# A decode attention step with its gradients and a gated MLP: the MLP moved whole to the front, weights laid out with neighbouring rows on a partition

## The chip, the core and the metric

The kernel runs on one core of a Trainium2 chip. The metric is device time in microseconds. Three runs of the kernel before took 745.66 to 747.29 us, median 746.24 us.

## What is computed

One token `x` (1 x 640) is normalised, goes through attention over a cache of 32 heads x 8192 positions x 128, and beside it through a gated MLP with 1728 hidden units. The output is the sum, and the kernel also returns the gradients of it, for a given `grad_out`, with respect to x, both caches and all five weight matrices.

```python
def _A_ref(x, k_cache, v_cache, wq, wo):
    q = (x @ wq).reshape(B, Sq, Hq, Dh).transpose(0, 2, 1, 3)
    scores = jnp.einsum("bhqd,bhkd->bhqk", q, k) * (Dh ** -0.5)
    p = _softmax(scores, axis=-1)
    o = jnp.einsum("bhqk,bhkd->bhqd", p, v)
    return o.transpose(0, 2, 1, 3).reshape(B, Sq, Hq * Dh) @ wo
...
xn = _layernorm(x, axis=-1)
return x + _A_ref(xn, k_cache, v_cache, wq, wo) + (silu(xn @ w1) * (xn @ w3)) @ w2
...
_out, _vjp = jax.vjp(_f, x, k_cache, v_cache, wq, wo, w1, w3, w2)
_grads = _vjp(grad_out)
```

All inputs and outputs are bf16. Each head reads 2 MB of K and 2 MB of V and writes 2 MB of dK and 2 MB of dV. wq and wo have 5.2 MB each, w1, w3 and w2 2.2 MB each, and each has a gradient of its own size.

## The kernel before

**Heads.** The outer loop (L480) is pipelined by one head: iteration h makes the scores of head h+1 and the outputs of head h. `product` (L271) forms S = K q and DP = V do: VectorE multiplies half a head of K or V by a row vector (L280), and TensorE sums over the head dimension by multiplying with the identity (L282). `outer` (L287) forms dV = p x do and dK = u x q in halves: VectorE makes 24 of 32 columns (L289), ScalarE the other 8 (L293), and Pool's queue issues the store (L295). `attend` (L326) and `dscores` (L345) contract V and K with one-column matmuls into `ob`.

**Loads.** All large loads go through SP's queue, in the order of the program. `load_k` and `load_v` (L108, L114) have three buffers each, so head h+3 is loaded once head h has been used (L503, L513). In front of the loop stand K0, wq and wo of group 0, V0, and K and V of heads 1 and 2 (L162 to L167).

**Groups.** Four heads share a group of wq and wo columns, loaded by `load_group` (L128) at the first head of the group before, into two buffers. `prep_steps` (L219) makes q (L224) and, by transposing wo (L234), do (L238) for the next group. `weights` (L348) uses a head's output vector: five one-column matmuls with wo (L357), then wo's buffer is overwritten with its own gradient on ScalarE (L359); the same for wq at the end of a group (L251). `finish_group` (L247) stores both. wq has 640 rows, of which a group is 1024 B each; a partition holds rows that lie 128 apart.

**The MLP.** It runs in four pieces of 432 hidden units. `load_piece` (L147) is called after heads 0, 5, 12 and 17, and `mlp_steps` (L377) is started at heads 3, 8, 15 and 20; its parts run in the gaps of the heads (`gap`, L472). A piece computes gate and up (L384), g times w2 (L387) and its sum (L390), some 15 small steps, a diagonal matrix (L430) from which TensorE and ScalarE make the row vectors broadcast to all partitions (L438, L441), the gradient of w2 in place (L443), and for w1 and w3 the product with the row vector (L452), its sum (L454) and the gradient in place (L456). The rows of w1 and w3 in a piece are 864 B long.

**Order.** VectorE, SP and Pool keep the order of the program (`ORDERED`, L58); the order of TensorE's and ScalarE's instructions is made by the framework's scheduler. `store` (L121) issues from Pool; stores of the last group but one and of the last MLP piece are put off (`late`) to head 30 (L487).

Of the kernel before, what the change touches and what calls it, by code (L numbers as in the profile page):

```python
# [9 lines left out]
BF16 = mybir.dt.bfloat16  # L10
F32 = mybir.dt.float32
# [5 lines left out]
P = 128  # L17
# [4 lines left out]
def kernel(  # L22
# [36 lines left out]
    NPIECE = 4  # L59
    ACT_J = 8  # L60
    scale = float(DH) ** -0.5
# [4 lines left out]
    mp = ctx.enter_context(tc.tile_pool(name="mlp", bufs=1))  # L66
# [14 lines left out]
    wq_v = A_wq.rearrange("(ci p) n -> p ci n", p=P)  # L81
    wo_v = A_wo.rearrange("(h p) c -> p h c", p=P)
    dwq_v = out_4.rearrange("(ci p) n -> p ci n", p=P)
    dwo_v = out_5.rearrange("(h p) c -> p h c", p=P)
    w1_v = B_w1.rearrange("(ci p) f -> p ci f", p=P)
    w3_v = B_w3.rearrange("(ci p) f -> p ci f", p=P)
    dw1_v = out_6.rearrange("(ci p) f -> p ci f", p=P)
    dw3_v = out_7.rearrange("(ci p) f -> p ci f", p=P)

    with tc.manual_schedule(engines=ORDERED):  # L90
# [7 lines left out]
        x_col_bf = consts.tile([P, NC], BF16, name="x_col_bf")  # L98
        g_col_bf = consts.tile([P, NC], BF16, name="g_col_bf")
        with nc.allow_non_contiguous_dma(reason="tiny column-layout loads of x / grad_out"):  # L100
            nc.sync.dma_start(x_col_bf[:], A_x.rearrange("a b (c p) -> p (a b c)", p=P))
            nc.scalar.dma_start(g_col_bf[:], grad_out.rearrange("a b (c p) -> p (a b c)", p=P))
# [25 lines left out]
        def load_group(g):  # L128
            hs = slice(g * GH * DH, (g + 1) * GH * DH)
            wq_g = wload.tile([P, NC, GH * DH], BF16, name="wq_g", tag="wq_g")  # L130
            nc.sync.dma_start(wq_g[:], wq_v[:, :, hs])
            wo_g = wload.tile([P, GH, D], BF16, name="wo_g", tag="wo_g")
            nc.sync.dma_start(wo_g[:], wo_v[:, g * GH:(g + 1) * GH, :])
            grp[g] = dict(wq=wq_g, wo=wo_g)

        assert F % NPIECE == 0
        FP = F // NPIECE
        pblocks = [(b0, min(P, FP - b0)) for b0 in range(0, FP, P)]
        NB = len(pblocks)
        NF = FP // P  # L140
        DRUN = 64
        DR1 = 48
        assert FP % DR1 == 0
        W1O, W3O, W2O = 0, NC * FP, 2 * NC * FP
        ml = {}

        def load_piece(pc):  # L147
            f0 = pc * FP
            wt = mp.tile([P, 2 * NC * FP + NB * D], BF16, name="wt", tag="wt")
            w1c = wt[:, W1O:W1O + NC * FP].rearrange("p (c f) -> p c f", c=NC)  # L150
            w3c = wt[:, W3O:W3O + NC * FP].rearrange("p (c f) -> p c f", c=NC)
            w2c = wt[:, W2O:W2O + NB * D].rearrange("p (b d) -> p b d", b=NB)
            if NB > NF:
                nc.gpsimd.memset(w2c[:, NF, :], 0.0)
            nc.sync.dma_start(w2c[:, 0:NF, :], B_w2[f0:f0 + NF * P, :].rearrange("(fb p) c -> p fb c", p=P))
            nc.sync.dma_start(w1c, w1_v[:, :, f0:f0 + FP])
            nc.sync.dma_start(w3c, w3_v[:, :, f0:f0 + FP])
            if NB > NF:
                nc.sync.dma_start(w2c[0:FP - NF * P, NF, :], B_w2[f0 + NF * P:f0 + FP, :])
            ml[pc] = (w1c, w3c, w2c)  # L160

        load_k(0)  # L162
        load_group(0)
        load_v(0)
        for h in range(1, min(3, H)):
            load_k(h)
            load_v(h)  # L167
# [18 lines left out]
        OUT0 = NC  # L186

# [3 lines left out]
        x_col = consts.tile([P, NC], F32, name="x_col")  # L191
        g_col = consts.tile([P, NC], F32, name="g_col")
# [5 lines left out]
        dxn_mlp = consts.tile([P, NC], F32, name="dxn_mlp")  # L198
        x_bc = tpool.tile([P, 2, D], F32, name="x_bc", tag="T")
# [10 lines left out]
        nc.vector.tensor_copy(x_col[:], x_col_bf[:])  # L210
        nc.vector.tensor_scalar(xn_col[:], x_col[:], negmean[:], rstd[:], ALU.add, ALU.mult)
        nc.vector.tensor_copy(XN_rep[:], xn_col[:].unsqueeze(2).to_broadcast([P, NC, P]))
        nc.vector.tensor_copy(g_col[:], g_col_bf[:])
        nc.vector.tensor_copy(G_rep[:], g_col[:].unsqueeze(2).to_broadcast([P, NC, P]))
        nc.vector.tensor_copy(xn_col_bf[:], xn_col[:])
        nc.vector.tensor_copy(xn2[:], xn_col[:].unsqueeze(2).to_broadcast([P, NC, 2]))


        def prep_steps(g):  # L219
# [24 lines left out]
            nc.scalar.copy(do_g[:].rearrange("p h d -> p (h d)"), ps_d[:])  # L244
            G_["do"] = do_g

        def finish_group(g):  # L247
            G_ = grp.pop(g)
            store(dwo_v[:, g * GH:(g + 1) * GH, :], G_["wo"][:], g == NG - 2)
            for ci in range(NC):  # L250
                nc.scalar.activation(G_["wq"][:, ci, :], G_["dqbc"][:].rearrange("p h d -> p (h d)"),  # L251
                                     ACTF.Copy, scale=xn_col[:, ci:ci + 1])
            store(dwq_v[:, :, g * GH * DH:(g + 1) * GH * DH], G_["wq"][:], g == NG - 2)
# [94 lines left out]
        def weights(st):  # L348
# [5 lines left out]
            odq_bf = small.tile([P, 2], BF16, name="odq_bf")  # L354
            nc.vector.tensor_copy(odq_bf[:], odq[:])
            for ci in range(NC):
                nc.tensor.matmul(accbank[:, OUT0 + ci:OUT0 + ci + 1], lhsT=G_["wo"][:, hh, ci * P:(ci + 1) * P],  # L357
                                 rhs=odq_bf[:, 0:1], start=False, stop=True, skip_group_check=True)
            nc.scalar.activation(G_["wo"][:, hh, :], g_bc_bf[:], ACTF.Copy, scale=odq[:, 0:1])  # L359
# [5 lines left out]
            for ci in range(NC):  # L365
                nc.tensor.matmul(accbank[:, DXN0 + ci:DXN0 + ci + 1], lhsT=wqT[:, ci * P:(ci + 1) * P],
                                 rhs=odq_bf[:, 1:2], start=False, stop=True, skip_group_check=True)
# [5 lines left out]
            if hh == GH - 1:  # L373
                finish_group(st.g)


        def mlp_steps(pc):  # L377
            f0 = pc * FP
            w1c, w3c, w2c = ml.pop(pc)
            gu_ps = ps_w.tile([P, 2, 8], F32, name="gu_ps", tag="w")  # L380
            for wi, wt in enumerate((w1c, w3c)):
                for bi, (b0, rows) in enumerate(pblocks):
                    for ci in range(NC):
                        nc.tensor.matmul(gu_ps[0:rows, wi, bi:bi + 1], lhsT=wt[:, ci, b0:b0 + rows],  # L384
                                         rhs=xn_col_bf[:, ci:ci + 1], start=(ci == 0), stop=(ci == NC - 1))
            T2 = tpool.tile([P, NB, D], BF16, name="T2", tag="T")
            nc.vector.tensor_tensor(T2[:], w2c, g_bc_bf[:].unsqueeze(1).to_broadcast([P, NB, D]), ALU.mult)  # L387
            dh_ps = ps_w.tile([P, NB, DRUN], F32, name="dh_ps", tag="w")
            for i in range(D // DRUN):
                nc.tensor.matmul(dh_ps[:], lhsT=ident_bf[:], rhs=T2[:, :, DRUN * i:DRUN * (i + 1)],  # L390
                                 start=(i == 0), stop=(i == D // DRUN - 1))
            yield
            gu = mp.tile([P, 2, NB], F32, name="gu")
            nc.vector.memset(gu[:], 0.0)
            for bi, (b0, rows) in enumerate(pblocks):
                if rows < P:
                    nc.vector.tensor_copy(gu[0:rows, :, bi:bi + 1], gu_ps[0:rows, :, bi:bi + 1])
            nc.vector.tensor_copy(gu[:, :, 0:NF], gu_ps[:, :, 0:NF])
            gate = gu[:, 0, :]
            up = gu[:, 1, :]  # L400
            th = mp.tile([P, NB], F32, name="th")
            nc.scalar.activation(th[:], gate, ACTF.Tanh, scale=0.5)
            yield
            dhc = mp.tile([P, NB], F32, name="dhc")
            nc.vector.tensor_reduce(dhc[:], dh_ps[:], AX.X, ALU.add)
            sig = mp.tile([P, NB], F32, name="sig")
            nc.vector.tensor_scalar(sig[:], th[:], 0.5, 0.5, ALU.mult, ALU.add)
            silu = mp.tile([P, NB], F32, name="silu")
            nc.vector.tensor_tensor(silu[:], gate, sig[:], ALU.mult)
            hcol = mp.tile([P, NB], F32, name="hcol")  # L410
            nc.vector.tensor_tensor(hcol[:], silu[:], up, ALU.mult)
            hcol_bf = mp.tile([P, NB], BF16, name="hcol_bf")
            nc.vector.tensor_copy(hcol_bf[:], hcol[:])
            for bi, (b0, rows) in enumerate(pblocks):
                for ci in range(NC):
                    nc.tensor.matmul(accbank[:, OUT0 + ci:OUT0 + ci + 1], lhsT=w2c[0:rows, bi, ci * P:(ci + 1) * P],
# [61 lines left out]
        for _ in prep_steps(0):  # L478
            pass
# [108 lines left out]
```

## Time and profile before

| | |
|---|---|
| runs, median (lowest to highest) | 746.24 us (745.66 to 747.29) |
| the profiled execution's own time | 747.42 us |
| its span, first to last instruction | 745.7 us |
| TensorE, VectorE, ScalarE, Pool busy | 75%, 86%, 62%, 13% |
| packets' time on the load queue / the store queue, share of 16 DMA engines | 49.7% / 49.5% |
| HBM read / written | 151.67 MB / 151.34 MB |
| granted TensorE clock, mean | 0.762 |

The span is the time between the first and the last instruction; the execution's own time has 1.7 us more around it. A group line of the profile names the source line, the engine, the operation, what is written and read, the shapes, the count, then the busy time in us, the mean of one in ns, and the idle time before. A DMA's issue takes well under 1 us on its queue; its data land later: 15.2 us for a K load, 15.7 us for a dK or dV store, 17.6 and 24.7 us for wq and wo loads (medians).

### The profile page before, as it was taken

The numbers are of one execution on the slowest core, as the hardware profiler recorded it, in microseconds if no ns is written. First come the engines' busy times: TensorE is split into PE (matmuls) and PEld (weight loads), VectorE is DVE, ScalarE is ACT, GpSimd is POOL, SyncE is SP. The second block draws the span as 40 slices with busy tenths as digits, with TensorE's granted clock in tenths as the row PEclk, the third lists the DMA queues.
The fourth block names the chain that finished last, engine by engine and source line by source line (L and its number), as shares of the span: only waits on it lengthen the run. The fifth ranks groups of instructions, "written<-read, shape, count | busy, mean of one in ns | idle before, by whom it ended". The sixth has DMA issues, their size and how long they took to land.

```text
span 745.7 us, 15906 instructions
## 1 busy us (share of the span) xinstructions
PE 561.7 (75%) x6444; PEld 327.8 (44%) x6451; DVE 639.4 (86%) x764; ACT 463.2 (62%) x1378; POOL 97.9 (13%) x172
## 2 busy tenths in 40 slices
PE   2788677878777887784887877777778765888872
PEld 1344354445454454442554444454444442544442
DVE  3799688997988979879588997988999877899993
ACT  3456656566775477663766566766477753766676
POOL 0010102111111101210102111110111200111312
PEclk9868857687887668777857688876798776985885
DMA  8999999999999999999999999999999999999997
GB/s 319 427 420 407 420 422 405 374 416 421 417 427 423 415 429 424 425 419 384 402 420 399 371 417 419 422 428 422 420 425 420 424 416 427 380 421 428 395 362 299
DMA packets 50205, 304.04 MB, mean 408 GB/s; under 512 B 5460, under 2 KB 21780, under 8 KB 25556
## 3 DMA queue, kind: packets, MB, share of 16 engines
q1 hardware_dynamic: 26612, 151.51, 49.7%
q0 software_dynamic: 22720, 151.35, 49.5%
q8 instruction: 50, 0.82, 0.4%
q10 hardware_dynamic: 800, 0.17, 0.1%
q14 instruction: 23, 0.19, 0.1%
HBM read 151.67 MB, written 151.34 MB: 406 GB/s over the span
## 4 chain that ended last, share of the span: by engine, by line
DMA 43%; DVE 28%; PE 17%; issue 7%; ACT 2%; SPq 1%; POOL 1%; POOLq 0%; DVEq 0%; ACTq 0%
DMA wo_g<-in_A_wo_dram 22%; DVE T L280 14%; DMA out_dram<-wq_g 9%; DVE ot L289 8%; PE psS L282 7%; DMA Kt<-in_A_k_cache_dram 6%; DMA out_dram<-ot 5%; PE psDP L282 3%; PE ob L326 2%; DMA wq_g<-in_A_wq_dram 1%; DVE S_sb L299 1%; PE ps_t L234 1%; ACT wt L443 1%; DVE DP_sb L333 1%; PE ps_d L238 1%
## 5 line engine op out<-in xcount | busy, mean ns | idle before, releaser
L282 PEld LDWEIGHTS <-ident_bf 128*128 128x128 bf16 x1024 | 123.7, 122 | 233.1 <-issue 183.7
L282 PE MATMUL psDP<-T,ident_bf 128*128 128x512 bf16 x512 | 177.2, 507 | 62.5 <-DVE T L280 62.5
L293 ACT ACTIVATE ot<-qs_g,Uf 128x128 bf16<-128x128 bf16 x512 | 153.9, 389 | 38.6 <-DVE Uf L343 26.0
L282 PE MATMUL psS<-T,ident_bf 128*128 128x512 bf16 x512 | 164.4, 476 | 16.5 <-DVE T L280 15.3
L280 DVE TENSOR_TENSOR T<-Kt,qs_g 128x4096 bf16<-128x4096 bf16 x64 | 146.4, 2289 | 26.5 <-DMA Kt<-in_A_k_cache_dram 9.8
L293 ACT ACTIVATE ot<-do_g,Pf 128x128 bf16<-128x128 bf16 x512 | 155.7, 390 | 9.3 <-DMA out_dram<-ot 8.6
L280 DVE TENSOR_TENSOR T<-Vt,do_g 128x4096 bf16<-128x4096 bf16 x64 | 146.0, 2281 | 0.0
L295 POOL DMA_DIRECT2D out_dram<-ot x128 | 68.8, 538 | 573.9 <-ACT ot L293 324.1
L289 DVE TENSOR_TENSOR ot<-do_g,P 128x3072 bf16<-128x3072 bf16 x64 | 112.3, 1755 | 8.6 <-DMA out_dram<-ot 7.4
L289 DVE TENSOR_TENSOR ot<-qs_g,U 128x3072 bf16<-128x3072 bf16 x64 | 112.0, 1752 | 4.9 <-DMA out_dram<-ot 4.9
L345 PEld LDWEIGHTS <-Kt 128*128 128x128 bf16 x2048 | 58.7, 99 | 17.6 <-issue 14.9
L359 ACT ACTIVATE wo_g<-g_bc_bf,odq 128x640 bf16<-128x640 bf16 x32 | 26.5, 827 | 59.7 <-PE accbank L357 59.7
L345 PE MATMUL ob<-U,Kt 128*128 128x1 bf16 x2048 | 57.5, 164 | 3.1 <-DVE U L340 2.8
L326 PEld LDWEIGHTS <-Vt 128*128 128x128 bf16 x2048 | 58.0, 99 | 0.0
L326 PE MATMUL ob<-P,Vt 128*128 128x1 bf16 x2048 | 56.7, 164 | 0.0
L369 ACT ACTIVATE dq_diag<-ident_bf,odq 128x128 bf16<-128x128 bf16 x32 | 12.9, 402 | 46.6 <-DVE odq L353 46.6
L236 ACT COPY woT<-ps_t 128x512 bf16<-128x512 bf16 x40 | 22.5, 581 | 24.4 <-PE ps_t L234 24.4
L299 DVE TENSOR_REDUCE S_sb<-psS 128x64 f32<-128x512 f32 x32 | 21.9, 685 | 18.1 <-PE psS L282 18.1
L234 PE MATMUL ps_t<-ident_bf,wo_g 128*128 128x128 bf16 x160 | 19.2, 257 | 19.8 <-DMA wo_g<-in_A_wo_dram 19.8
L311 ACT ACTIVATE E<-S_sb,negM 128x64 f32<-128x64 f32 x32 | 11.1, 347 | 33.9 <-DVE negM L308 33.9
L336 PE MATMUL sm<-rdot,ones_f 128*128 128x1 f32 x64 | 12.1, 258 | 20.7 <-DVE E L335 20.7
L303 PE MATMUL sm<-ident_f,mrow 128*128 128x128 f32 x64 | 18.7, 380 | 10.7 <-DVE mrow L301 10.5
(122 smaller groups left out, 502.2 us busy)
## 6 DMA issues: line engine op xcount, KB each, us to landing
out_dram<-ot POOLq DMA_DIRECT2D x128, 1024.0 KB, 15.7
Kt<-in_A_k_cache_dram SPq DMA_DIRECT2D x32, 2048.0 KB, 15.2
Vt<-in_A_v_cache_dram SPq DMA_DIRECT2D x32, 2048.0 KB, 12.9
wq_g<-in_A_wq_dram SPq DMA_DIRECT2D x8, 640.0 KB, 17.6
wo_g<-in_A_wo_dram SPq DMA_DIRECT2D x8, 640.0 KB, 24.7
out_dram<-wo_g POOLq DMA_DIRECT2D x8, 640.0 KB, 17.5
out_dram<-wq_g POOLq DMA_DIRECT2D x8, 640.0 KB, 17.1
wt<-in_B_w_dram SPq DMA_DIRECT2D x8, 540.0 KB, 25.3
```

What stands on the lines that cost most here:

```text
L234: nc.tensor.transpose(ps_t[:, hh * DH:(hh + 1) * DH], wo_g[:, hh, ci * P:(ci + 1) * P], ident_bf[:])
L236: nc.scalar.copy(woT[:], ps_t[:])
L280: nc.vector.tensor_tensor(T[:], src[:, :, ds_], vec[:, ds_].unsqueeze(1).to_broadcast([P, J, DHH]), ALU.mult)
L282: nc.tensor.matmul(ps[:], lhsT=ident_bf[:], rhs=T[:, :, RUN * i:RUN * (i + 1)], start=(half == 0 and i == 0), stop=(half == 1 and i == DHH ...
L289: nc.vector.tensor_tensor(ot[:, 0:JD], vec.rearrange("p (a b) -> p a b", b=2).unsqueeze(1).to_broadcast([P, JD, DH // 2, 2]), w2[:, j0:j0 ...
L293: nc.scalar.activation(ot[:, j].rearrange("p a b -> p (a b)"), vec, ACTF.Copy, scale=wf[:, half, j - JD:j - JD + 1])
L295: nc.gpsimd.dma_start(dst[h][:, j0:j0 + JH, :], ot[:].rearrange("p j a b -> p j (a b)"))
L299: nc.vector.tensor_reduce(st.S[:], st.ps["S"][:], AX.X, ALU.add)
L303: nc.tensor.matmul(st.sm[:, 8:8 + P], lhsT=mrow[:].to_broadcast([P, P]), rhs=ident_f[:], start=True, stop=True, skip_group_check=True)
L326: mm = nc.tensor.matmul(st.ob[:, 0:1], lhsT=st.V[:, j, :], rhs=st.P2[:, j, 0:1], start=(j == 0), stop=(j == J - 1), skip_group_check=True)
L345: nc.tensor.matmul(st.ob[:, 1:2], lhsT=st.K[:, j, :], rhs=st.U2[:, j, 0:1], start=(j == 0), stop=(j == J - 1), skip_group_check=True)
L359: nc.scalar.activation(G_["wo"][:, hh, :], g_bc_bf[:], ACTF.Copy, scale=odq[:, 0:1])
```

## The change

Three things change together.

1. **Layouts.** wq, w1 and w3 are viewed so that partition p holds rows 5p to 5p+4; wo so that a partition holds four neighbouring rows of a group; w2 so that each of 108 partitions holds 16 neighbouring rows. The columns of x and xn follow ("pm" forms beside "cm" ones), and they are made by 20 one-column matmuls from the broadcast rows rather than by two DMAs.
2. **Groups.** wq is loaded and stored for eight heads at a time (2048 B rows), wo still for four. As a partition of wo now holds rows of one head next to each other, o is spread by a selection matrix: per head a small ScalarE activation and one f32 matmul into `on_ps`, and once per group `finish_wo` with all 20 matmuls and four ScalarE copies. The wq stores of the last two groups are issued for each group.
3. **The MLP** is one piece, ahead of head 0. w2 lies in three output buffers (tag "o"), w1 and w3 in two of the three K buffers, so K1 and K2 are loaded after the MLP's stores. The pool `mlp` is gone.

```diff
-        load_k(0)
-        load_group(0)
-        load_v(0)
-        for h in range(1, min(3, H)):
-            load_k(h)
-            load_v(h)
+        for rows in (6, 5, 5):
+            w2c = opool.tile([P, rows, D], BF16, name="w2c", tag="o")
+            nc.sync.dma_start(w2c[0:FR], w2_v[:, r0:r0 + rows, :])
...
+        w1t = kvpool.tile([P, NC, F], BF16, name="w1t", tag="K")
+        nc.sync.dma_start(w1t[:], w1_v)
+        w3t = kvpool.tile([P, NC, F], BF16, name="w3t", tag="K")
+        nc.sync.dma_start(w3t[:], w3_v)
+        load_k(0)
+        load_wq(0)
+        load_wo(0)
+        load_v(0)
+        load_v(1)
+        load_v(2)
...
+        mlp = mlp_steps()
+        next(mlp)
+        next(mlp)
         for _ in prep_steps(0):
             pass
+        for _ in mlp:
+            pass
+        load_k(1)
+        load_k(2)
```

```diff
+    wq_v = A_wq.rearrange("(p ci) n -> p ci n", ci=NC)
+    wo_v = A_wo.rearrange("(g p r) c -> g p r c", p=P, r=GH)
+    w1_v = B_w1.rearrange("(p ci) f -> p ci f", ci=NC)
+    w2_v = B_w2.rearrange("(q r) c -> q r c", r=R2)
...
+        def finish_wo(g):
...
+            for r in range(GH):
+                for ci in range(NC):
+                    nc.tensor.matmul(accbank[:, OUT0 + ci:OUT0 + ci + 1], lhsT=wo_g[:, r, ci * P:(ci + 1) * P],
+                                     rhs=on_bf[:, r:r + 1], start=False, stop=True, skip_group_check=True)
+                nc.scalar.activation(wo_g[:, r, :], g_bc_bf[:], ACTF.Copy, scale=on[:, r:r + 1])
+            store(dwo_v[g], wo_g[:], g == NG - 2)
...
-            for ci in range(NC):
-                nc.tensor.matmul(accbank[:, OUT0 + ci:OUT0 + ci + 1], lhsT=G_["wo"][:, hh, ci * P:(ci + 1) * P],
-                                 rhs=odq_bf[:, 0:1], start=False, stop=True, skip_group_check=True)
-            nc.scalar.activation(G_["wo"][:, hh, :], g_bc_bf[:], ACTF.Copy, scale=odq[:, 0:1])
+            om = small.tile([P, GH], F32, name="om")
+            nc.scalar.activation(om[:], rmask[:], ACTF.Copy, scale=odq[:, 0:1])
+            nc.tensor.matmul(G_["on_ps"], lhsT=sel[:, hh, :], rhs=om[:], start=(hh == 0), stop=(hh == GH - 1),
+                             skip_group_check=True)
+            if hh == GH - 1:
+                finish_wo(st.g)
```

The MLP itself, its sums over w2 first (R2 = 16, FR = 108):

```diff
+            for r0, rows, w2c in w2_parts:
+                T2 = tpool.tile([P, rows, D], BF16, name="T2", tag="T")
+                nc.vector.tensor_tensor(T2[0:FR], w2c[0:FR], g_bc_bf[0:FR].unsqueeze(1).to_broadcast([FR, rows, D]), ALU.mult)
...
+            for wi, wt in enumerate((w1t, w3t)):
+                wr = wt[:].rearrange("p c (q r) -> p c r q", r=R2)
+                for r in range(R2):
                     for ci in range(NC):
+                        nc.tensor.matmul(gu_ps[0:FR, wi, r:r + 1], lhsT=wr[:, ci, r, :],
                                          rhs=xn_col_bf[:, ci:ci + 1], start=(ci == 0), stop=(ci == NC - 1))
...
+            for r0, rows, w2c in w2_parts:
+                for r in range(rows):
...
+                    nc.scalar.activation(w2c[0:FR, r, :], g_bc_bf[0:FR, :], ACTF.Copy, scale=hcol[:, r0 + r:r0 + r + 1])
+                nc.gpsimd.dma_start(dw2_v[:, r0:r0 + rows, :], w2c[0:FR])
...
+            for wi, (wt, dst) in enumerate(((w1t, dw1_v), (w3t, dw3_v))):
+                for c0 in range(0, NC, 2):
...
+                    nc.vector.tensor_tensor(T[:], wt[:, c0:c0 + n, :],
+                                            bc_sb[:, wi, :].unsqueeze(1).to_broadcast([P, n, F]), ALU.mult)
...
+                nc.gpsimd.dma_start(dst, wt[:])
```

At the end, dx is stored from its own tile in 10 B pieces on SP's queue, and the output row on ScalarE's.

## The prediction, made before the changed kernel had run

> **What bounds the kernel now.** I read the page's engine table first: VectorE 86%, TensorE 75%, no engine full. Then the page's slices, where the DMA row is:
>
> ```profile
> DMA  8999999999999999999999999999999999999997
> GB/s 319 427 420 407 420 422 405 374 416 421 417 427 423 415 429 424 425 419 384 402 420 399 371 417 419 422 428 422 420 425 420 424 416 427 380 421 428 395 362 299
> DMA packets 50205, 304.04 MB, mean 408 GB/s; under 512 B 5460, under 2 KB 21780, under 8 KB 25556
> ```
>
> The 16 DMA engines are busy from the second slice to the last but one, yet the bytes per second vary: busy engines carry 420 to 429 GB/s in most slices and 362 to 384 in a few. So the bound is the DMA engines' time, and some of it goes to something other than bytes. The windows view tells what (columns: stretch in us, its length, five engines' busy time and count, TensorE clock, DMA share, GB/s):
>
> ```profile
> 5.00:20.00 15.00, 6.54 (x32) 3.73 (x33) 8.29 (x14) 5.73 (x10) 0.00 (x0) 1.00 1.02 402
> 20.00:35.00 15.00, 10.96 (x49) 4.75 (x46) 11.11 (x11) 5.64 (x14) 0.00 (x0) 0.89 1.02 434
> 80.00:125.00 45.00, 32.48 (x312) 18.45 (x310) 33.82 (x47) 23.37 (x66) 5.30 (x9) 0.66 1.01 426
> 125.00:145.00 20.00, 15.55 (x175) 9.18 (x174) 19.61 (x24) 13.33 (x41) 4.81 (x7) 0.67 0.98 358
> 405.00:425.00 20.00, 15.42 (x173) 9.04 (x171) 19.57 (x25) 13.11 (x41) 4.83 (x7) 0.67 0.96 348
> 535.00:595.00 60.00, 48.04 (x582) 28.13 (x582) 57.11 (x63) 41.70 (x127) 8.08 (x14) 0.84 1.01 423
> 700.00:720.00 20.00, 16.55 (x185) 9.14 (x185) 19.64 (x22) 12.76 (x42) 6.90 (x10) 0.76 0.99 369
> ```
>
> The reader is to see that stretches of nearly only K and V run at 423 to 426, loads alone at 434, and that the slow ones, at the same DMA share, are those in which the DMA issues of the timeline are w1, w3, w2, wq and wo. VectorE has room: in the timeline its order repeats every 18.81 us per head when nothing stops it (L280 at 35.29 and at 54.10), 602 us for 32 heads.
>
> **Part 1, larger rows (a gain).** The trace's packet records give loads of 864 B 41.2 ns each (5120, w1 and w3), of 1024 B 46.6 ns (5120, wq) and of 16384 B 624.5 ns (8192, K and V). A line through the last two is 8.1 ns + bytes/26.6 per ns. The 1280 B rows of wo and w2 take 58.1 ns. After the change loads have rows of 2048 B (wq), 5120 B (wo), 17280 B (w1, w3), 7680 and 6400 B (w2). By the line, as a share of 16 engines: wq 14.9 to 13.6 us, wo 14.9 to 12.8, w1 and w3 13.2 to 10.5, w2 6.3 to 5.3: 7.1 us less. The stores' packets are counted differently, but show bytes per ns and engine: 23.3 (wq), 24.6 (wo, w2), 20.2 (w1, w3) against 26.2 for the 8192 B of dK and dV. Brought to 24 for wq and to 26 for the others, the stores save 4.8 us. The two column loads of x and grad_out (1280 packets of 2 B, 0.7 us) go. Sum **12.6 us**; I take 13. The windows bound it from above: against 424 GB/s, every slow stretch after 35 us (the three above, 350:365 at 356, 630:645 at 370 and six at 411 to 419) loses 17.7 us in all. From below, 8: wq stays at 2 KB, and the stores may not follow the loads.
>
> **Part 2, the MLP ahead of head 0 (a loss).** Its VectorE work is not new; its place is. Today head 0 and its stores begin here:
>
> ```profile
> 16.11 4.49 DVE L280 TENSOR_TENSOR T<-Kt,qs_g 128x4096 bf16<-128x4096 bf16 x2 [3.87 <-ACT qs_g L227]
> 35.42 0.68 POOL L295 DMA_DIRECT2D out_dram<-ot  x1 [33.60 <-DVE E L335]
> ```
>
> So 19.3 us lie from a head's first product to its first store. Until 35.4 us the queue lives on loads that wait for nothing: K, V of three heads. The change puts 6.64 MB of w2, w1, w3 ahead of them and takes K1 and K2 out, whose two buffers w1 and w3 hold. The MLP's durations scale from these groups (line, engine, shapes, count | busy us, mean ns | idle):
>
> ```profile
> L384 PEld LDWEIGHTS <-wt 128*128 128x128 bf16 x120 | 4.1, 102 | 1.2 <-issue 1.1
> L387 DVE TENSOR_TENSOR T<-wt,g_bc_bf 128x2560 bf16<-128x2560 bf16 x4 | 5.9, 1484 | 0.0
> L430 DVE TENSOR_TENSOR diag<-ident_bf,dgu 128x1024 bf16<-128x1024 bf16 x4 | 2.8, 692 | 0.1
> L441 ACT CAST bc_sb<-bc_ps 128x432 bf16<-128x432 f32 x8 | 3.6, 505 | 0.0
> L452 DVE TENSOR_TENSOR T<-wt,bc_sb 128x2160 bf16<-128x2160 bf16 x8 | 10.2, 1280 | 0.0
> L456 DVE TENSOR_TENSOR wt<-bc_sb,xn 128x2160 bf16<-128x2160 bf16 x8 | 10.3, 1283 | 0.3
> ```
>
> Step by step, in us from the span's start:
> - x, its mean and the column forms end at 12.3 as now (L216 ends at 12.24); the new selection tables lie in VectorE's wait for x before 5.1, and 20 one-column matmuls replace two casts.
> - w1 has landed at 14.5 and w3 at 19.7: 0.46 MB at 5.0 (0:5 ran at 92 GB/s), then 420 GB/s.
> - dh: three products, 16 x 640 elements by L387's 1484 ns per 2560: 5.9. Between them VectorE waits for ten matmuls (2.25 as L390 x10 in the timeline) and a reduction (0.55, scaled from L405): 8.4. End 26.6.
> - gate and up: 160 matmuls, now with 108 weight columns that lie 16 elements apart, which no row shows. Lower end: 41 ns each, as 40 of L384 take 1.65 in the timeline, loads overlapping. Upper end: 270 ns, the f32 weight load of L312. I take 102 ns, one load of L384 with no overlap, the nearest row without it. From 14.5, 80 for w1 (8.2) and dh's 30 (6.8) end at 29.5, 80 more at **37.7**. With 41 ns they are hidden beside dh and end at 27; with 270 at 64.5.
> - tanh, nine small VectorE steps (0.16 each), a cast, diag (3456 elements, 2.3) and four casts of bc (0.505 each) with hand-offs: 7.5, to 45.2.
> - Two matrices, each 8640 elements by L452 and again by L456 (5.1 + 5.1) and 1 of waiting for TensorE to free a T buffer: 22.4. Head 0's first product at **67.6**, its first store at **87**.
>
> What the queue can do until 87: loads w 6.64 MB, K0, V0 to V2 8.39, wq of two groups 1.31, wo 0.66; stores of w 6.64; K1 and K2 4.19, each behind the landing of a w store. That is 27.8 MB, 66 us of work: **some 20 us idle**. SP is blocked at K1 meanwhile, with nothing behind it that could run; Pool stands with w1's store behind w2's last, 16 scaled copies at 0.82 each.
>
> *A rule against this step.* The Trainium skill, "TensorE: Matmul & The Clock Gate", section on weight-path perf modes, keeps the fast weight load for 128 columns, and its LDWEIGHTS section gives columns/1.2 ns, an estimate of 90 ns for 108. By that the end would be 2 us earlier than by mine. "SBUF — State Buffer" adds that access stepping to a new 16-byte line each time pays a penalty, without a figure; it would be later. The trace has no such load. "DMA: Bandwidth & Descriptors" would also put 108 partitions on 12 of 16 engines; no row here shows it; w2 would land 2 us later, beside the x chain.
>
> **Part 3, wo by selection.** Per head one f32 matmul and a 128x4 activation replace five matmuls and one 0.83 us copy; at a group's end four copies come together. ScalarE is 62% busy, TensorE 75%: hidden in the stream, behind DMA. If ScalarE's cover were gone, 3 us per group. In the last group there is none: at 730 to 740 ScalarE is busy 9.3 of 10. Three more copies at 0.828 (L359) and two small ones at 0.2: **+2.9**; 0 if the scheduler puts wq first. In the stream SP waits for wo's store alone instead of wq's (62.4 us, four times, in the waits of SP); the DMA engines are busy at those times, so I cost it at nothing, and the next thing late is the same saturated queue.
>
> **The sum.** Now: 13.0 MB moved at 35.4, so 291.0 MB in 710.3 us. With 13 us less for those bytes, 276.2 MB take (710.3 - 13) x 276.2/291.0 = 661.8. After: 87 + 661.8 + 2.9 = 751.7 span. The profiled execution took 747.42 for a span of 745.7, and the median of the runs, 746.24, is 1.2 below it: 751.7 + 1.7 - 1.2 = **752**.
>
> **Rivals.**
> 1. *Faster*: strided weight loads overlap as today's do. Head 0 starts at 57, first store at 76, sum 741; with 18 us gained, 736. For it: 39 loads in 1.56 us now, clock 1.0 at the start. Against: columns are no longer neighbours. It decides from a first store before about 80 us.
> 2. *Much slower*: 270 ns per load, first store at 114, sum 779; at 180 ns, 764. For it: L312. Against: that is f32.
> 3. *The rows grow and the packets' time does not* (the engines cut them again): no 13 us, 764. Against: the line through 1 KB and 16 KB.
>
> **Chances.** Forecast, 746 to 759: 0.50. Rival 1: 0.25. Rival 2: 0.20. Rival 3: 0.05. The range 739 to 771 leaves out the far halves of rivals 1 and 2. A measurement can tell 0.2% from no change, 1.5 us: faster (under 744.7) 0.25; within, the forecast's lower edge, 0.10; slower 0.65.
>
> **What would show it.** Right: GB/s near 420 in all middle slices and none under 400; DMA share well under 1 between 45 and 87 us; the first dV store near 87; gate and up matmuls near 102 ns apart; packets under 2 KB down from 21780 to some 4500. Wrong: a first store before 80, DMA full from the start, middle slices still at 350 to 380, or a tail that is no longer than now.

## The result, and the profile after

After: 812.09 us median (810.99 to 814.27, 4 runs); before, beside it on the same chip, 746.62. The ratio is 1.0882, 95% interval 1.0855 to 1.0908: 8.8% slower. The direction was the forecast's, the size was not: 752 was forecast, and the range ended at 771. The profiled execution took 812.53 for a span of 810.4.

The page of the kernel after, its slices (a slice is now 20.3 us):

```profile
DMA  8940377999999999999999999999999999999977
GB/s 256 424 175 1 110 280 262 406 431 422 424 418 429 427 423 401 429 411 423 418 421 431 427 369 424 397 395 423 418 428 429 423 413 426 373 427 397 418 324 273
DMA packets 35771, 304.04 MB, mean 375 GB/s; under 512 B 3818, under 2 KB 4074, under 8 KB 10610
```

The packets under 2 KB are down from 21780 to 4074, as forecast. The slow slices have not gone from the middle (369, 373, 395), and a hole has opened at the front: from the third slice to the seventh the DMA engines are partly or wholly idle. The windows view (columns as before) has the same in three stretches:

```profile
60.00:115.00 55.00, 24.45 (x232) 18.07 (x234) 22.98 (x23) 31.40 (x33) 2.40 (x4) 0.94 0.27 95
150.00:780.00 630.00, 485.68 (x5697) 286.21 (x5703) 548.60 (x595) 419.22 (x1289) 70.43 (x130) 0.77 1.00 417
780.00:810.40 30.40, 11.98 (x192) 8.40 (x191) 15.68 (x30) 19.70 (x58) 4.02 (x7) 0.62 0.66 259
```

The middle is as full as before's, which moves 415 GB/s:

```profile
40.00:700.00 660.00, 512.57 (x5934) 300.06 (x5940) 581.34 (x679) 418.66 (x1257) 84.72 (x146) 0.76 1.01 415
```

So most of the loss must be at the front. VectorE's timeline there (start, busy, engine, line, operation, count, and in brackets the idle time ahead of it and what ended it; the last line is Pool's):

```profile
60.42 0.19 DVE L430 COPY sm_f<-gu_ps 108x32 f32<-108x32 f32 x1 [31.50 <-PE gu_ps L425]
72.71 3.83 DVE L474 TENSOR_TENSOR T<-w1t,bc_sb 128x3456 bf16<-128x3456 bf16 x2 [7.71 <-ACT bc_sb L457]
98.52 1.06 DVE L474 TENSOR_TENSOR T<-w1t,bc_sb 128x1728 bf16<-128x1728 bf16 x1 [21.97 <-PE dx_ps L477]
115.50 4.48 DVE L306 TENSOR_TENSOR T<-Kt,qs_g 128x4096 bf16<-128x4096 bf16 x2
134.47 0.53 POOL L321 DMA_DIRECT2D out_dram<-ot  x1 [18.62 <-DVE E L361]
```

Three idle times are to be seen: 31.5 us for gate and up, 7.7 for the broadcast rows, and 22.0 for one sum of w1's products. Head 0 begins at 115.5 and its first store goes out at 134.5; 67.6 and 87 were forecast. What ends the three is in the timeline of all engines, of which these are TensorE's and ScalarE's lines:

```profile
28.18 16.09 PE L425 MATMUL gu_ps<-xn_col_bf,w1t 128*108 128x1 bf16 x80
44.13 16.25 PE L425 MATMUL gu_ps<-xn_col_bf,w3t 128*108 128x1 bf16 x80
65.31 14.73 ACT L457 CAST bc_sb<-bc_ps 128x432 bf16<-128x432 f32 x8 [4.46 <-PE bc_ps L455]
79.52 11.79 ACT L466 ACTIVATE w2c<-g_bc_bf,sm_f 108x640 bf16<-108x640 bf16 x16
91.67 1.08 ACT L244 COPY woT<-ps_t 128x512 bf16<-128x512 bf16 x2
92.32 0.58 PE L246 MATMUL ps_d<-woT,G_rep 128*128 128x512 bf16 x1 [11.64 <-ACT woT L244]
95.29 1.00 PE L477 MATMUL dx_ps<-T,ident_bf 128*128 128x192 bf16 x5
```

The 160 matmuls of gate and up are 200 ns apart (16.09 us for 80). The eight broadcast copies take 14.7 us. And the sums that VectorE waits for (L477) stand on TensorE behind a matmul of `prep_steps(0)` (L246); that waits for a ScalarE copy (L244), and this stands on ScalarE behind the eight broadcast copies and 16 copies for w2's gradient. VectorE needs none of these w2 copies; it waits for them through two queues.

### The profile page after: what moved, and what is told of

Its sections match the earlier page's. It is cut to its first block, busy times and chain, and to the rows that moved or that the text cites. A ratio compares the mean times of both kernels' runs of the same rounds, so it can differ in the third digit from the quotient of the medians.

```text
span 810.4 us, 15979 instructions
## 1 busy us (share of the span) xinstructions
PE 589.7 (73%) x6529; PEld 364.5 (45%) x6537; DVE 631.7 (78%) x703; ACT 486.6 (60%) x1423; POOL 80.7 (10%) x154
## 2 busy tenths in 40 slices
DMA packets 35771, 304.04 MB, mean 375 GB/s; under 512 B 3818, under 2 KB 4074, under 8 KB 10610
## 4 chain that ended last, share of the span: by engine, by line
DVE 40%; DMA 30%; PE 16%; ACT 7%; issue 6%; POOL 0%; POOLq 0%; DVEq 0%; ACTq 0%; SPq 0%
DVE T L306 18%; DMA out_dram<-ot 16%; DVE ot L315 14%; DMA wo_g<-in_A_wo_dram 10%; PE gu_ps L425 4%; DMA out_dram<-wo_g 4%; PE psS L308 3%; PE psDP L308 3%; DVE S_sb L325 2%; ACT wo_g L267 2%; ACT wq_g L273 2%; ACT bc_sb L457 2%; ACT w2c L466 1%; PE dh_ps L417 1%; PE ob L352 1%
## 5 line engine op out<-in xcount | busy, mean ns | idle before, releaser
L308 PE MATMUL psDP<-T,ident_bf 128*128 128x512 bf16 x512 | 179.4, 514 | 60.1 <-DVE T L306 60.1
L319 ACT ACTIVATE ot<-do_g,Pf 128x128 bf16<-128x128 bf16 x512 | 155.9, 390 | 12.0 <-DMA out_dram<-ot 11.2
L308 PE MATMUL psS<-T,ident_bf 128*128 128x512 bf16 x512 | 155.7, 457 | 9.7 <-DVE T L306 9.4
L371 PEld LDWEIGHTS <-Kt 128*128 128x128 bf16 x2048 | 59.2, 100 | 14.4 <-issue 11.8
L383 ACT ACTIVATE om<-rmask,odq 128x4 f32<-128x4 f32 x32 | 9.5, 297 | 54.5 <-DVE odq L379 54.5
L402 ACT CAST dqbc_g<-ps_db 128x128 bf16<-128x128 f32 x32 | 8.5, 266 | 48.8 <-PE ps_db L401 48.7
L362 PEld LDWEIGHTS sm<-rdot,ones_f 128*128 128x128 f32 x64 | 11.4, 213 | 53.7 <-DVE E L361 53.4
L361 DVE SCALAR_TENSOR_TENSOR E<-DP_sb,P 128x64 f32<-128x64 f32 x32 | 7.2, 226 | 30.2 <-ACT Pf L346 27.1
```

The costliest lines, as they stand in the source:

```text
L308: nc.tensor.matmul(ps[:], lhsT=ident_bf[:], rhs=T[:, :, RUN * i:RUN * (i + 1)], start=(half == 0 and i == 0), stop=(half == 1 and i == DHH ...
L319: nc.scalar.activation(ot[:, j].rearrange("p a b -> p (a b)"), vec, ACTF.Copy, scale=wf[:, half, j - JD:j - JD + 1])
L362: nc.tensor.matmul(st.sm[:, 4:5], lhsT=ones_f[:], rhs=rdot[:], start=True, stop=True, skip_group_check=True)
L371: nc.tensor.matmul(st.ob[:, 1:2], lhsT=st.K[:, j, :], rhs=st.U2[:, j, 0:1], start=(j == 0), stop=(j == J - 1), skip_group_check=True)
```

## The experiments

The first three take one suspect each.

**w2_apart.** w2's rows lie 108 apart on a partition again, so that the weight columns are neighbours and the broadcast copies write neighbouring elements:

```diff
-    w2_v = B_w2.rearrange("(q r) c -> q r c", r=R2)
+    w2_v = B_w2.rearrange("(r q) c -> q r c", r=R2)
...
-                wr = wt[:].rearrange("p c (q r) -> p c r q", r=R2)
+                wr = wt[:].rearrange("p c (r q) -> p c r q", r=R2)
...
-                    nc.scalar.copy(bc_sb[:, wi, :].rearrange("p (q r) -> p r q", r=R2)[:, r0:r0 + RC, :], bc_ps[:])
+                    nc.scalar.copy(bc_sb[:, wi, :].rearrange("p (r q) -> p r q", r=R2)[:, r0:r0 + RC, :], bc_ps[:])
```

> The changed kernel with w2's rows laid 108 apart on a partition (row r*108+q on partition q) in place of 16 neighbours; so the weight columns of gate and up, and the broadcast rows written by ScalarE, are contiguous. Theory A (three stalls at the start, one for one to the end; gate and up and the ScalarE copies are slow because of the 32 byte step): the 160 gate and up matmuls fall from 200 ns apart to about 41, gate and up end near 35 us in place of 60, the eight copies from 1.84 us apart to 0.5, head 0 starts near 80 in place of 115.5, time near 777. Rival B (108 columns in place of 128 are what makes the load slow): matmuls stay at 200 ns apart, only the copies gain, time near 800. Rival C (the loss lies in the stream, in wo's selection and wq by eight heads, and the start is caught up later): head 0 starts earlier and the time stays within 5 us of 812.

Measured: 783.07 us (one run). The timelines of VectorE and ScalarE:

```profile
42.77 0.19 DVE L430 COPY sm_f<-gu_ps 108x32 f32<-108x32 f32 x1 [14.35 <-PE gu_ps L425]
47.67 3.48 ACT L457 CAST bc_sb<-bc_ps 128x432 bf16<-128x432 f32 x8 [4.46 <-PE bc_ps L455]
69.10 1.06 DVE L474 TENSOR_TENSOR T<-w1t,bc_sb 128x1728 bf16<-128x1728 bf16 x1 [15.79 <-PE dx_ps L477]
86.08 4.48 DVE L306 TENSOR_TENSOR T<-Kt,qs_g 128x4096 bf16<-128x4096 bf16 x2
```

The layout cost 17.6 us in gate and up and 11.2 in the copies (14.73 to 3.48). Neighbouring columns do not bring the loads to the expected 41 ns: 14.4 us of waiting for 160 are still some 90 ns each. The third wait is still there, 15.8 us.

**prep_after.** Head 0's `prep_steps` are written after the MLP's last part:

```diff
-        for _ in prep_steps(0):
-            pass
         for _ in mlp:
             pass
+        for _ in prep_steps(0):
+            pass
```

> The changed kernel with the preparation of group 0 (q and do) written after the MLP instead of between its parts, so that on TensorE the sums for dx come ahead of the transposes that wait for ScalarE. Theory A: the 22.0 us wait of VectorE for TensorE before the third product with w1 falls to 1 to 2 us, head 0 starts near 95, time near 791. Rival D (VectorE waits there for TensorE's speed and not for its order): the wait stays near 20 and so does the time, 812. Rival C: head 0 earlier, time within 5 us of 812.

Measured: 793.98 us (one run). VectorE's timeline:

```profile
79.07 1.06 DVE L474 TENSOR_TENSOR T<-w1t,bc_sb 128x1728 bf16<-128x1728 bf16 x1 [3.58 <-PE dx_ps L477]
95.94 4.48 DVE L306 TENSOR_TENSOR T<-Kt,qs_g 128x4096 bf16<-128x4096 bf16 x2
```

The wait falls from 22.0 to 3.6 and head 0 comes 19.6 us earlier. So the order of two loops in the program, with nothing computed differently, cost 18 us.

**gu_forms.** The 160 loads in four forms of 40, a measurement:

```diff
+                    n, step = (FR, 16) if r < 8 else (P, 13)
                     for ci in range(NC):
+                        if wi == 0:
+                            lw = wt[:, ci, r * 100:r * 100 + n]
+                        else:
+                            lw = wt[:, ci, r:r + step * (n - 1) + 1:step]
+                        nc.tensor.matmul(gu_ps[0:n, wi, r:r + 1], lhsT=lw,
```

> A measurement of weight loads inside the changed kernel; gate and up take other columns than they should, so the values are not those of the model: w1's loads are contiguous and w3's step over 16 columns (108 columns) or 13 (128 columns), half of each with 108 and half with 128 columns. If the step makes a load slow: w1 near 41 ns apart with both counts, w3 near 200 with both. If the count does: 108 columns near 200 and 128 near 41, with or without a step. If both are needed: only w3 with 108 is slow. Time by theory A, a step alone: 16 us less than 812, near 796.

Measured: 793.41 us (one run). The groups by form (w1 neighbours, w3 with a step; the busy time over the count is the spacing, as the matmuls overlap):

```profile
L429 PE MATMUL gu_ps<-xn_col_bf,w3t 128*108 128x1 bf16 x40 | 8.2, 340 | 0.0
L429 PE MATMUL gu_ps<-xn_col_bf,w1t 128*108 128x1 bf16 x40 | 3.8, 231 | 0.0
L429 PE MATMUL gu_ps<-xn_col_bf,w3t 128*128 128x1 bf16 x40 | 2.5, 198 | 0.0
L429 PE MATMUL gu_ps<-xn_col_bf,w1t 128*128 128x1 bf16 x40 | 1.2, 165 | 0.0
```

128 neighbouring columns: 30 ns; 108 neighbouring: 95; 128 with a step of 13 elements: 63; 108 with a step of 16: 205. In these four forms the width counts threefold and the step twofold, and they multiply. Neither alone explains the 200 ns.

**w2_apart_prep_after.** Both edits.

> Both edits, of w2_apart and of prep_after, together. Theory A: they add up, head 0 starts near 66 us, as the forecast had it, and the time is near 764; what is then still above the forecast of 752 lies in the stream. Rival C: the time stays above 800. Rival E (once the first stall is gone the next hides behind the same wait): the gains overlap, the time is near 775.

Measured: 770.86 us median (769.53 to 772.44), ratio 1.0329 (1.0309 to 1.0349). 41 of the 66 us are back. Head 0 begins at 71.31, and the first store is at 91.78. The next runs start from this kernel.

**gu_128_columns.** On it, 128 columns in place of 108:

```diff
-                        nc.tensor.matmul(gu_ps[0:FR, wi, r:r + 1], lhsT=wr[:, ci, r, :],
+                        nc.tensor.matmul(gu_ps[:, wi, r:r + 1], lhsT=wt[:, ci, r * 100:r * 100 + P],
```

> A measurement on w2_apart_prep_after (its edits, and one more): the gate and up matmuls read 128 neighbouring columns of w1 and w3, r*100 to r*100+127, in place of 108. What it leaves out: gate and up are then not the model's, and the gradients that depend on them are not either; the work is otherwise the same. The 160 weight loads should then take 30 ns each, 4.8 us, where 108 neighbouring columns took 14.4, so that head 0's first product comes up to 9.6 us earlier, near 62, if nothing else is late. Theory D (the time goes one for one with head 0's start): about 9 us less than w2_apart_prep_after, 759 to 764. Rival (the delay left at the front is by now covered by the loads, about 57 us of transfers that lie before head 0 anyway): within 2 us of it, 769 to 773.

Measured: 761.34 us (759.11 to 761.71), ratio 1.0194 (1.0174 to 1.0214). VectorE's timeline:

```profile
32.11 0.19 DVE L429 COPY sm_f<-gu_ps 108x32 f32<-108x32 f32 x1 [3.75 <-PE gu_ps L424]
60.43 4.48 DVE L306 TENSOR_TENSOR T<-Kt,qs_g 128x4096 bf16<-128x4096 bf16 x2
```

Head 0 comes 10.9 us earlier and the time falls by 9.5: nearly one for one, as theory D had it.

**own_tile_for_E, wo_per_head, wq_four_heads.** Three suspects in the stream, each alone on w2_apart_prep_after: `row_dots` writes a tile of its own, wo as before without the selection, wq four heads at a time.

```diff
-            nc.vector.scalar_tensor_tensor(st.E[:], st.DP[:], 1.0, st.P2[:, :, 0], ALU.mult, ALU.mult, accum_out=rdot[:])
+            Ej = small.tile([P, J], F32, name="Ej")
+            nc.vector.scalar_tensor_tensor(Ej[:], st.DP[:], 1.0, st.P2[:, :, 0], ALU.mult, ALU.mult, accum_out=rdot[:])
```

```diff
-    wo_v = A_wo.rearrange("(g p r) c -> g p r c", p=P, r=GH)
+    wo_v = A_wo.rearrange("(g r p) c -> g p r c", p=P, r=GH)
```

```diff
-    GW = 8
+    GW = 4
```

> Based on w2_apart_prep_after (770.9 us). VectorE's product at row_dots writes a tile of its own in place of E, so that it no longer waits for ScalarE's Pf to have read E (25.4 us in 7 waits there, one at each group's end, behind the four wo and five wq copies). Theory F (the burst of finish_wo at a group's end stops VectorE, and with it the stores, and the DMA engines run short): these waits go and the time falls by 5 us or more, to 766 or less. Rival G (the DMA queue catches up, since the rest of the head has slack; the loss is in the larger transfers of eight heads of wq): the waits go and the time stays within 2 us.

> Based on w2_apart_prep_after (770.9 us). wo as in the kernel before: rows 128 apart (1280 B), no selection matmul, per head five matmuls and one ScalarE copy. Theory F: VectorE's waits for Pf fall to a few us, the end loses its 2.9 us of extra copies, and against that the wo rows cost about 3 us more of DMA time: time near 764. Rival G: only the end's 3 us against 3 us of rows: 771.

> Based on w2_apart_prep_after (770.9 us). wq in groups of four heads (1024 B rows) as before, rows still neighbours. Rival G: the large wq transfers go and the time falls to 766 or less in spite of 2 us more for the smaller rows. Theory F: 772 to 773, the price of the smaller rows alone.

Measured: 772.13 (768.84 to 772.91), ratio 1.0341 (1.0317 to 1.0365); 770.88 (770.14 to 772.06), 1.0337 (1.0320 to 1.0355); 773.07 (772.83 to 773.37), 1.0362 (1.0347 to 1.0378). The first is a lesson in waits. VectorE's waits (total us, times, longest), in w2_apart_prep_after:

```profile
DVE ot L315 <- DMA out_dram<-ot: 33.2, 21, 7.9
DVE E L361 <- ACT Pf L346: 25.4, 7, 5.0
```

and in own_tile_for_E:

```profile
DVE ot L315 <- DMA out_dram<-ot: 71.2, 37, 6.6
```

The wait for ScalarE is gone and the one for a store's landing has grown by more. The DMA engines set the pace, and VectorE waits for them at one place or another. wo's rows of 5120 B with their selection are worth nothing that can be seen. Rival G's 771 came, but its gain of 3 us by the rows does not show: the packets' time on the two queues is 735.5 us with the long rows and 734.4 with the short ones. With wq four heads at a time the time is 2.2 us longer, as theory F had it, but not where shorter rows would show it: between the first store and 60 us before the end the queue moves 418 GB/s, against 414 in w2_apart_prep_after. The difference lies at the ends: head 0 begins 1.5 us later (72.8), and the last 60 us move 292 GB/s against 332, with one put-off store of wq there instead of two. So it is not shown to be a gain of the rows.

**before_no_mlp and after_no_mlp.** What is left out in both is the MLP with its three gradients; the second has the changed wq and wo in before's order of K and V.

```diff
-        mlp_load = {0: 0, 5: 1, 12: 2, 17: 3}
-        mlp_start = {3: 0, 8: 1, 15: 2, 20: 3}
+        mlp_load = {}
+        mlp_start = {}
+        nc.vector.memset(dxn_mlp[:], 0.0)
```

> The kernel before without its MLP: no load, no arithmetic and no store of w1, w3, w2 (three gradients and the MLP's part of the output and of dx are left out), 13.3 MB less. Theory S (the MLP's traffic costs its bytes, 31 us at 424 GB/s, and the slow stretches around it are caught up): 715. Theory R (its small rows and the stretches they slow cost some 9 us more, as the windows of before read): 706.

> The changed stream without the MLP (the same is left out): wq by eight heads with neighbouring rows, wo with neighbouring rows and the selection, K and V of three heads loaded ahead as before. To be read against before_no_mlp. By the prediction's part 1 and 3 (wq and wo rows win 4 to 5 us, the end loses 2.9): 2 us faster than it. Theory J (with the MLP gone a saturated queue gains the packets' time in full, and the end's copies run beside the last stores): 4 to 6 us faster. Theory L (stalls at the group ends take it): 3 us or more slower.

Measured: 713.47 us (712.93 to 714.45), ratio 0.9560 (0.9545 to 0.9576); 713.71 (712.74 to 716.23), ratio 0.9569 (0.9542 to 0.9596). The timelines at head 0, of before_no_mlp:

```profile
15.98 4.49 DVE L280 TENSOR_TENSOR T<-Kt,qs_g 128x4096 bf16<-128x4096 bf16 x2 [4.22 <-ACT qs_g L227]
33.81 0.68 POOL L295 DMA_DIRECT2D out_dram<-ot  x1 [31.99 <-DVE E L335]
```

and of after_no_mlp:

```profile
17.77 4.49 DVE L323 TENSOR_TENSOR T<-Kt,qs_g 128x4096 bf16<-128x4096 bf16 x2 [5.04 <-ACT qs_g L252]
36.03 0.69 POOL L338 DMA_DIRECT2D out_dram<-ot  x1 [34.21 <-DVE E L378]
```

Inside the stream the MLP costs 746.3 - 713.5 = 33 us in before, which is its 13.3 MB at 406 GB/s (before runs at 408 over the span), so its short rows add next to nothing. After_no_mlp is 2 us shorter behind head 0 (the spans are 711.9 and 712.0, less 15.98 and 17.77), and its later start takes them back. These 2 us are not a faster queue: by the pages the packets of the two queues take 98.1% of one span and 98.2% of the other.

**before_long_mlp_rows.** Before, with each MLP piece loaded and stored as one row of 4320 B on a partition; these are then other elements than the piece's, so the MLP's values and gradients are not the model's.

```diff
-            nc.sync.dma_start(w1c, w1_v[:, :, f0:f0 + FP])
+            nc.sync.dma_start(wt[:, W1O:W1O + PX], w1_v[:, pc * PX:(pc + 1) * PX])
```

> The kernel before with the same number of bytes in each piece of the MLP, but loaded and stored as one contiguous row of 4320 B per partition (864 B and 1280 B rows before): the pieces then hold other elements of w1, w3 and w2, so the MLP's values are not those of the model. Theory R: 5 us by the packets' line, up to 9 by the windows: 737 to 741. Theory S: within 2 us of 746.

Measured: 744.91 us (743.29 to 747.12, 10 runs), ratio 0.9982 (0.9969 to 0.9994). The packets' own time on the two queues, over 16 engines, fell by 6.3 us (99.2% of 745.7 to 98.7% of 743.1, 739.7 to 733.4), and the piece loads' issues on SP stand 22 us in all instead of 94 (16 issues before, 12 now; SP's timeline). The kernel's time fell by 1.4.

**mlp_pieces_wo_neighbours_2.** The changed layouts of x, wq (four heads), wo, w1 and w3 with before's four pieces, where before has them; the MLP's diagonal matrix lies in an output buffer:

```diff
-    wo_v = A_wo.rearrange("(h p) c -> p h c", p=P)
-    w1_v = B_w1.rearrange("(ci p) f -> p ci f", p=P)
+    wo_v = A_wo.rearrange("(g p r) c -> g p r c", p=P, r=GH)
+    w1_v = B_w1.rearrange("(p ci) f -> p ci f", ci=NC)
```

> The part of the change that concerns the stream, alone: the MLP in four pieces within heads 3 to 24 as before, wo with four neighbouring rows and the selection, wq, w1 and w3 with rows 5p to 5p+4 but groups of four heads and pieces of 432 columns, so only wo's rows grow; the MLP's diagonal matrix lies in an output buffer, for room. Theory F: 2 to 3 us of DMA time are won on wo, 3 are lost at the end and some at the group ends: 747 to 753. Rival H (rows gain and the burst is hidden): 743 to 746.

Measured: 757.95 us (755.47 to 759.87), ratio 1.0153 (1.0121 to 1.0185), which neither theory gave. VectorE's waits:

```profile
DVE T L323 <- DMA Kt<-in_A_k_cache_dram: 47.4, 4, 15.5
```

K loads came late. In SP's timeline one piece's issues stand long, with V and K behind them:

```profile
163.24 0.55 SPq L164 DMA_DIRECT2D wt<-in_B_w_dram  x1
163.84 20.91 SPq L165 DMA_DIRECT2D wt<-in_B_w_dram  x1
184.85 12.63 SPq L167 DMA_DIRECT2D wt<-in_B_w_dram  x1
```

The 16 piece loads stand 110 us in all, but 94 in before too, where VectorE waits 9.8 us for K. What differs is the longest of them, 20.9 us against 11.3. Which of the edits makes K late was not separated and stays open.

## Why the prediction was wrong

**One table carries it.** Head 0's first product, the first store and the span, in us, from the timelines and pages; "rest" is span less first product.

| kernel | product | store | span | rest |
|---|---|---|---|---|
| after | 115.5 | 134.5 | 810.4 | 694.9 |
| gu_forms | 98.2 | 117.1 | 791.3 | 693.1 |
| prep_after | 95.9 | 117.1 | 791.9 | 696.0 |
| w2_apart | 86.1 | 104.7 | 780.9 | 694.8 |
| w2_apart_prep_after | 71.3 | 91.8 | 769.4 | 698.1 |
| gu_128_columns | 60.4 | 82.0 | 759.3 | 698.9 |
| after_no_mlp | 17.8 | 36.0 | 712.0 | 694.2 |
| before_no_mlp | 16.0 | 33.8 | 711.9 | 695.9 |
| before (MLP within) | 16.1 | 35.4 | 745.7 | 729.6 |

However long the front takes, the rest is 693 to 699 us in the kernels without the MLP in the stream (698.4, 696.9 and 698.6 in own_tile_for_E, wo_per_head and wq_four_heads). What the front delays, the end is late by, nearly in full: from after to gu_128_columns head 0 begins 55.1 us earlier and the span is 51.1 shorter. This is the prediction's own shape (a first store, then a saturated stream), and it held; the terms put into it failed. From 751.7 to 810.4 there are 58.7 us: 47.5 to the first store (134.5 against 87: terms 1 to 3, less 0.3 from first product to first store) and 11.2 behind it (675.9 against 661.8 + 2.9: terms 4 and 5).

1. **Gate and up, "I take 102 ns": +22.7.** They ended at 60.4, not 37.7. A load took 200 ns, between the bounds of 41 and 270, which is 15.7 us of it. The other 7 are the start: nothing lay beside dh, and TensorE began at 28.2, after dh's sums. The landing of w1 at 14.5 was wrong too:

```profile
w1t<-in_B_w_dram SPq DMA_DIRECT2D x1, 2160.0 KB, 20.0
w3t<-in_B_w_dram SPq DMA_DIRECT2D x1, 2160.0 KB, 24.5
```

   Issued at 2.4 and 3.0, they landed at 22.4 and 27.5; the queue moved 265 and 256 GB/s in 5:10 and 10:15, not 420. w2's layout, chosen for long rows, had put a step of 16 elements into the weights; 108 columns did the rest (gu_forms). Rival 2 had such slow loads; at its 180 ns it gave 764, because the later start and the next three terms were missing there as well.
2. **"Four casts of bc (0.505 each)": +4.8.** Writing 2-byte elements 32 B apart, the eight took 14.73 us, 1841 ns apart; with neighbours 3.48, 435 apart (w2_apart). First product of w1 at 72.7, 12.3 after gate and up instead of 7.5.
3. **"1 of waiting for TensorE to free a T buffer": +20.4.** For w1 it was 22.0, for w3 1.3; VectorE's own work was a little shorter than forecast. The prediction asked what is queued behind SP and Pool, but not what stands ahead of the sums on TensorE and ScalarE. prep_after shows the cause.
4. **"Rows gain 12.6, I take 13": about 0.** Before's pace without any gain gives 710.3 x 276.2/291.0 = 674.2 for what follows the first store; it took 675.9. The first step that failed is from rows to the packets' time. After's page has for the load and the store queue:

```profile
q1 hardware_dynamic: 13928, 151.51, 46.0%
q0 software_dynamic: 21616, 151.35, 45.1%
```

   That is 91.1% of 810.4, 738.3 us; before it was 99.2% of 745.7, 739.7. The packets' time fell by 1.4 us, not by 12.6 (the prediction's own figures for the stores add up to 4.5 rather than 4.8, so 12.3). By the packet records wq's and wo's loads took what the line gives (84 ns for 2048 B, 197 for 5120 B), but those of w1 and w3 took 745 ns where the line gives 658, wo's stores gained nothing (211 ns for 5120 B, 208 before), and K's and V's packets took 633 ns each instead of 624.5, which alone is 4.4 us. Why, no run shows. Rival 3, held at 0.05, had this term.

   The second step that failed is from packets to time: 6.3 us less of packets' time gave 1.4 in before_long_mlp_rows. Nor does the pace follow the rows: between the first store and 60 us before the end, before runs at 414 GB/s, before_no_mlp at 420, after_no_mlp, with longer rows, at 417, after at 415. That the slow stretches were the small rows' price was wrong: the middle has slow slices still, with the MLP's rows gone from it and those of wq and wo grown. What makes them slow is not shown.
5. **The tail, "+2.9": nothing that reaches the end.** The copies came as forecast: the last wq store is issued 7.9 us after the last head's last store in w2_apart_prep_after and 5.4 in wo_per_head, without the selection. But from that head store to the end are 14.7 and 15.2 us. After's end is slower than before's (259 GB/s in the last 30 us, 325 before), yet before_no_mlp, with wo as before, has 260 there too. This fits the MLP's last stores, which before puts off to head 30 and after no longer has there.

Right were 19.3 us from first product to first store (19.0), dh's end to some 2 us (28.9 for 26.6), w1's and w3's VectorE work, the DMA engines' idle time at the front (in kind: 0.27 in 60:115; in all it was 43% of 134.5 us, not some 20 us), and the packets under 2 KB. "None under 400" in the middle was wrong.

**The two rules in the record.** By the Trainium skill, "TensorE: Matmul & The Clock Gate", section on weight-path perf modes, 108 columns lose the fast weight load, and the figure of its LDWEIGHTS section gave an estimate of 90 ns; the 95 ns of 108 neighbouring columns against 30 of 128 agree. "SBUF — State Buffer", specifications, has a penalty for stepping to a new 16-byte line each time. The runs have a factor of two on TensorE's loads with steps of 26 and 32 B, and of four on ScalarE's writes 32 B apart (1841 against 435 ns); that the lines are the reason, no run shows. The prediction held the two as alternatives, one lowering and one raising the price; in this kernel they multiply. No run here shows the rule on 12 engines for 108 partitions.

**What the MLP's place costs.** Within the stream 33 us. Ahead of it, by the times against after_no_mlp (713.71), 98 as written, 57 with both edits and 48 in gu_128_columns. No kernel here with the MLP at the front comes under before.

## What to carry to other kernels

Work moved ahead of a saturated stream cost nearly its whole latency here, so add up its chain on every in-order engine, including what another routine has put ahead of it there; inside the stream it cost only its bytes. A layout that lengthens a DMA's rows also sets the step with which the engines read and write: look at the weight columns and the copies it leaves before counting the rows' gain. A slow stretch that coincides with small packets is not yet their price; take the packets away and time it, and look whether the packets' time fell.

## What was not expected of the hardware

- One-column matmuls with bf16 weights, spacing at a granted clock of 1.00 (0:60 of gu_forms): 30 ns (128 neighbouring columns), 95 (108 neighbouring), 63 (128, step 13), 205 (108, step 16).
- A ScalarE copy of 128x432 f32 to bf16: 435 ns apart when it writes neighbours, 1841 with elements 32 B apart (means of one: 559 and 2264).
- An issue on SP's queue is not always under 1 us, as the section on the profile before has it: the 16 piece loads of before stand up to 11.3 us each. In before_long_mlp_rows they stand 22 us instead of 94 and the time falls by only 1.4.
- 6.3 us less of packets' time on 16 busy engines shortened the kernel before by 1.4 us.
- From 50205 packets to 35771, for the same 304.04 MB, the packets' time on the two queues fell by 1.4 us (739.7 to 738.3).
